# Windowed attention and FFN in one planned kernel: flag, branch hints, last output, plan slack and the third pair's loads

## The chip, the cores and the metric

The kernel runs on one core of a Trainium2 chip. The metric is the device time of one execution in microseconds, the median over the runs shown. Each execution of the program computes the whole result. TensorE is called PE in the rows, its weight loads PEld; VectorE is DVE, ScalarE is ACT, GpSimd is POOL and SyncE is SP. A "q" behind an engine's name means an instruction of its sequencer (a wait, a branch, a DMA issue).

## The reference

Attention with a window and sink keys over four batches, eight heads, 768 positions and 64 dimensions, and behind it a feed-forward network (FFN) over the 3072 tokens, 512 wide with 2048 hidden units:

```
scores = q @ k.T / sqrt(64)
keep = (pos_k < n_sink) | ((pos_q - pos_k >= 0) & (pos_q - pos_k < window))
a = softmax(where(keep, scores, -1e9))          # n_sink = 4, window = 128
x = (a @ v), heads side by side                 # 3072 x 512
h = x @ w_in
g = where(h >= 1, h, where(h <= -1, 0, (h + 1)**2 / 4))
out = g @ w_out
```

All inputs are float32; q and k come with factors of about 30, so the softmax is sharp. The weights reach the kernel as 64-bit words that it decodes itself.

## The kernel before

The work is cut into eight chunks of 384 tokens (four batches, first and second half of the sequence). For each chunk the attention of eight heads writes the tile `xn`, and then the FFN of this chunk runs while the attention of the next is computed. The first half's heads (16 of the 64 units) are computed in pairs of heads (`pair_load`, `pair_scores`, `pair_sums`, `early_transp`, `pair_r`, `pair_av`), the first four of them in `first_pairs` ahead of everything else; the others are single units (`load`, `scores`, `values`, `transp`, `av`, `sinks`), split into a high and a low part for the product. `pair_load` (L610) brings keys (L616) and queries (L618) of a pair into the rings `ks_ring` and `qh_ring` of two buffers each. The rings `ql_ring` (two buffers) and `kr_ring` (one) are used by the units alone, from 16 on. `pair_values` (L621) loads V into one of two buffers `vq`.

The FFN of a chunk is a loop over 16 blocks of hidden units (`NJ`). `stage1` (L827) makes twelve products (L835) for a block; ACT and VectorE turn the result into g, with a high part `gh` (L846) and a low part `gl` (L847); `stage2` (L850), two blocks later, makes nine products (L858) into three output banks. With the last block, ACT copies each bank (L869) and SP stores it (L871). `split` (L873) makes the high and low part of x (L875, L876). `block` (L320) loads and decodes two weight blocks: the transfer (L359), two byte instructions (L361, L363), a combination (L365), a copy on ACT (L367) and a subtraction (L368).

All of this is not issued as it is written: each step hands `Plan.op` an engine, a guessed time in ns, a function, and what it reads and writes. `Plan.due` works out a due time for each operation from TensorE's order, and `Plan.order` plays the engines against each other: an engine takes the ready operation that is due first; SP takes a transfer no sooner than some microseconds before it is due; for TensorE there are two lanes, A (attention) and B (FFN), each in its own order, and `turn` says which lane's head comes next. If both are ready, the lane whose share of the chunk's work is behind has its turn:

```
ka, kb = ("A", a.group[1]), ("B", b.group[1])
return a if done[ka] * LEAD * total[kb] <= done[kb] * total[ka] else b
```

The instructions are issued in the order that comes out, and the engines wait for one another by semaphores. The order is made on the host; the chip does not change it.

The kernel is right in this form for inputs in a certain range (a sink count up to 4, a window from 1 to 128, scores below a bound, weights whose exponents lie in a range). `checks` (L957 to L969, VectorE) puts these conditions into `flag`; a transpose on TensorE (L978) brings the 128 partitions into one row, and `result` (L971 to L974) makes the integer `other` of it. Before, these steps form a group of their own after the last chunk. `values_load` (L1030) loads `other` into a register on each engine, and each engine branches (L1031): if it is 0, past a block of code that computes everything again in a general way; the block behind `tc.If` is not entered for these inputs. Behind it come waits for all semaphores and the barrier at the end (L1031, L1098).

## Time and profile before

| | |
|---|---|
| time, median of 3 runs | 689.83 us (688.82 to 690.71) |
| time of the profiled execution | 689.68 us |
| its span, first to last instruction | 688.0 us |
| PE busy | 671.2 us (98%) |
| PEld busy | 601.7 us (87%) |
| DVE busy | 501.6 us (73%) |
| ACT busy | 489.2 us (71%) |
| POOL busy | 237.3 us (34%) |
| mean granted TensorE clock | 0.998 of full speed |

The span lies inside the profiled execution's time; 1.7 us are around it. A busy share is an average over stages with different limits, so the views by stretch and in order of time say more than this table. In a view of waits "X <- Y" means that the engine's instruction X was idle until Y was done. Matmuls are pipelined, so their times overlap. Register, branch and semaphore instructions do not count as busy.

### The profile page before, as it was taken

The page shows a single profiled execution, that of the slowest core. Times are in us where ns is not written, and L with a number is a line of the kernel's source. Part 1 is how long each engine was busy: PE and PEld are TensorE (multiplying, and loading weights), DVE is VectorE, ACT ScalarE, POOL GpSimd, SP SyncE. Part 2 cuts the span into 40 slices and gives each one's busy share as a digit, 9 for nine tenths or more (in the row PEclk, how much of TensorE's full clock was granted, in tenths as well). Part 3 has the DMA queues.
Part 4 walks back from the last instruction along what each step waited for, and adds up shares of the span by engine and source line. Part 5 has one row for each costly group of instructions (what it writes and reads, how often), then busy time and mean ns, then how long its engine had stood idle before and what let it go on. Part 6 is the DMA issues. An engine that isn't in the chain of part 4 may idle for free.

```text
span 688.0 us, 11934 instructions
## 1 busy us (share of the span) xinstructions
PE 671.2 (98%) x3853; PEld 601.7 (87%) x3853; DVE 501.6 (73%) x1421; ACT 489.2 (71%) x1245; POOL 237.3 (34%) x421
## 2 busy tenths in 40 slices
PE   6899999999999999999999999999999999999995
PEld 5688888889999999999999999999999999999994
DVE  6998999787767688686786877787787776733221
ACT  6887877777668777887778777797777866544332
POOL 3000014444433445453543454354453444300000
PEclk9999999999999999999999999999999999999999
DMA  6946433231223433434434433434424221000001
GB/s 220 333 170 240 141 143 117 60 92 49 61 65 117 126 110 126 142 98 145 128 93 147 123 105 128 135 118 134 124 89 123 67 89 43 1 31 16 1 0 51
DMA packets 41086, 73.94 MB, mean 107 GB/s; under 512 B 4344, under 2 KB 25656, under 8 KB 41016
## 3 DMA queue, kind: packets, MB, share of 16 engines
q1 hardware_dynamic: 41016, 73.09, 33.4%
q8 instruction: 33, 0.54, 0.3%
q14 instruction: 37, 0.30, 0.1%
HBM read 66.78 MB, written 6.29 MB: 106 GB/s over the span
## 4 chain that ended last, share of the span: by engine, by line
PE 87%; DVE 7%; ACT 2%; DMA 1%; issue 1%; POOL 0%; SPq 0%; POOLq 0%; DVEq 0%
PE o_ps L858 36%; PE h_ps L835 36%; PE ps_a L587 5%; PE ps_a L444 5%; PE ps_a L525 2%; DMA w<-w_in 1%; PE ps_a L656 1%; DVE wi L368 1%; PE ps_a L722 1%; DVE gl L847 1%; DVE x L876 1%; DVE ends L363 1%; ACT p L452 1%; DVE ends L361 1%; DVE w L365 1%
## 5 line engine op out<-in xcount | busy, mean ns | idle before, releaser
L835 PE MATMUL h_ps<-x,wi 128*128 128x384 f32 x1536 | 311.8, 340 | 0.8 <-DVE x L876 0.6
L835 PEld LDWEIGHTS h_ps<-x,wi 128*128 128x128 f32 x1536 | 262.5, 188 | 10.4 <-issue 2.0
L858 PE MATMUL o_ps<-w,gh 128*128 128x512 f32 x768 | 243.4, 398 | 0.0
L858 PE MATMUL o_ps<-w,gl 128*128 128x512 f32 x384 | 151.0, 393 | 0.0
L858 PEld LDWEIGHTS o_ps<-w,gh 128*128 128x128 f32 x768 | 134.1, 188 | 15.8 <-issue 1.5
L844 DVE SCALAR_TENSOR_TENSOR g<-g,h_ps 128x384 f32<-128x384 f32 x128 | 70.4, 550 | 67.1 <-ACT g L843 66.3
L842 ACT ACTIVATE g<-h_ps,half 128x384 f32<-128x384 f32 x128 | 73.9, 577 | 54.1 <-PE h_ps L835 53.2
L847 DVE TENSOR_TENSOR gl<-g,gh 128x384 fp32r<-128x384 f32 x128 | 77.0, 602 | 29.4 <-ACT gh L846 28.8
L452 ACT ACTIVATE p<-p,peak 128x260 f32<-128x260 f32 (+1 forms) x144 | 71.6, 497 | 37.2 <-DVE peak L449 35.0
L846 ACT CAST gh<-g 128x384 fp32r<-128x384 f32 x128 | 65.3, 510 | 45.1 <-DVE g L844 43.9
L426 POOL TENSOR_TENSOR q_l<-r,q_h 128x384 fp32r<-128x384 f32 x48 | 50.6, 1053 | 116.9 <-ACT q_h L425 116.8
L858 PEld LDWEIGHTS o_ps<-w,gl 128*128 128x128 f32 x384 | 72.0, 188 | 16.9
L449 DVE CUSTOM_DVE_ANT_0 p<-ps_a,m 128x260 f32<-128x260 f32 (+1 forms) x144 | 57.7, 408 | 21.7 <-PE ps_a L444 21.4
L843 ACT ACTIVATE g<-g 128x384 f32<-128x384 f32 x128 | 67.2, 525 | 3.2
L471 DVE CUSTOM_DVE_ANT_0 p<-p,stat 128x128 f32<-128x128 f32 x128 | 60.1, 496 | 2.3
L546 POOL TENSOR_SCALAR_AFFINE_SELECT pt<-pt 128x384 fp32r<-128x384 f32 (+1 forms) x96 | 49.1, 514 | 23.7 <-ACT pt L534 12.6
L498 POOL TENSOR_TENSOR v_s<-r,v_s 128x256 fp32r<-128x256 f32 (+1 forms) x48 | 36.2, 754 | 60.1 <-ACT v_s L497 59.0
L551 POOL TENSOR_SCALAR_AFFINE_SELECT pt<-pt 128x384 fp32r<-128x384 f32 (+1 forms) x96 | 50.4, 545 | 0.2
L587 PEld LDWEIGHTS ps_a<-pt,v_s 128*128 128x128 f32 x304 | 42.5, 188 | 2.5 <-POOL v_s L498 0.2
L444 PE MATMUL ps_a<-k_s,q_l 128*128 128x260 f32 (+1 forms) x144 | 40.7, 283 | 1.3 <-POOL q_l L426 1.1
L587 PE MATMUL ps_a<-pt,v_s 128*128 128x256 f32 (+1 forms) x304 | 41.9, 275 | 0.0
L444 PE MATMUL ps_a<-k_s,q_h 128*128 128x260 f32 (+1 forms) x144 | 39.6, 275 | 0.0
(161 smaller groups left out, 851.6 us busy)
## 6 DMA issues: line engine op xcount, KB each, us to landing
r<-qk SPq DMA_DIRECT2D x48, 192.0 KB, 2.4
k_r<-qk SPq DMA_DIRECT2D x32, 262.0 KB, 2.8
w<-w_in SPq DMA_DIRECT2D x8, 1024.0 KB, 7.5
again<-w_in SPq DMA_DIRECT2D x16, 512.0 KB, 4.1
again<-w_out SPq DMA_DIRECT2D x16, 512.0 KB, 3.8
w<-w_out SPq DMA_DIRECT2D x6, 1024.0 KB, 8.5
out<-o SPq DMA_DIRECT2D x23, 256.0 KB, 2.4
r<-vx SPq DMA_DIRECT2D x32, 128.0 KB, 2.1
```

The costliest lines, as they stand in the source:

```text
L444: nc.tensor.matmul(ps()[:, lo:260], lhsT=q()[:, i * P:(i + 1) * P], rhs=k_s()[:, c0:c0 + 260 - lo], start=(j == 0), stop=(j == len(qs) - 1))
L449: op(DVE, 215 if lo else 350, lambda: nc.vector.tensor_tensor_reduce(out=p()[:, i, lo:260], in0=ps()[:, lo:260], in1=m, scale=-0.125, scal ...
L452: op(ACT, 400 if lo else 500, lambda: nc.scalar.activation(p()[:, i, lo:260], p()[:, i, lo:260], AF.Exp, bias=peak[:, n, i:i + 1], scale=-1.0,
L471: nc.vector.tensor_tensor_reduce(out=own, in0=own, in1=p()[:, k, 0:P], scale=r, scalar=0.0, op0=ALU.add, op1=ALU.add, accum_out=stat()[:, ...
L587: nc.tensor.matmul(z, lhsT=w, rhs=y, start=(n == 0), stop=(n == len(mms) - 1))
L835: nc.tensor.matmul(h_ps()[:, :T], lhsT=w_i[j][:, w, ct * P:(ct + 1) * P], rhs=x()[:, y, ct], start=(ct == 0 and n == 0), stop=(ct == NCT - ...
L842: op(ACT, 490, lambda: nc.scalar.activation(g(), h_ps()[:, :T], AF.Relu, bias=half, scale=0.5), r=[h_ps], w=[g])
L843: op(ACT, 440, lambda: nc.scalar.activation(g(), g(), AF.Square), w=[g])
L844: op(DVE, 470, lambda: nc.vector.scalar_tensor_tensor(g(), g(), 1.0, h_ps()[:, :T], op0=ALU.min, op1=ALU.max), r=[h_ps], w=[g])
L846: op(ACT, 420, lambda: nc.scalar.copy(gh(), g()), r=[g], w=[gh])
L847: op(DVE, 500, lambda: nc.vector.tensor_tensor(gl(), g(), gh().bitcast(F32), op=ALU.subtract), r=[g, gh], w=[gl])
L858: nc.tensor.matmul(ps(), lhsT=gg()[:, tt * P:(tt + 1) * P], rhs=w_o[j][:, w], start=(j == 0 and n == 0), stop=(j == NJ - 1 and n == 2))
```

## The change

Five things are changed. `checks` and `result` move into a step `decide` of lane A, put in the middle of the last chunk's FFN steps. A hint, one instruction on each engine, is placed in the last chunk behind the low part of block 13 of 16; it belongs to the branch, which now has a label, and to the jump past the general block. The last of the 24 output tiles is copied and stored in two halves of 256 columns: ACT copies and stores the first, VectorE copies and SP stores the second. `turn` gets a slack: where both lanes' heads are ready and the preferred one has been ready for less than 800 ns of the plan, but the other for 800 ns or more, the other has the turn. And the third pair's queries and keys go into a buffer of `ql_ring` and the one of `kr_ring`. The bodies of `checks` and `result` are as before.

```diff
--- before.py
+++ after.py
@@ -44,6 +44,7 @@
 SOON = 40000
+SLACK = 800
@@ -145,7 +146,8 @@ turn(t)
                 ka, kb = ("A", a.group[1]), ("B", b.group[1])
-                return a if done[ka] * LEAD * total[kb] <= done[kb] * total[ka] else b
+                x, y = (a, b) if done[ka] * LEAD * total[kb] <= done[kb] * total[ka] else (b, a)
+                return y if x.ready + SLACK > t >= y.ready + SLACK else x
@@ -612,7 +614,7 @@ pair_load(m)
-        q_h, k_h = qh_ring.new(), ks_ring.new()
+        q_h, k_h = (ql_ring.new(), kr_ring.new()) if m == 2 else (qh_ring.new(), ks_ring.new())
@@ -846,6 +848,8 @@ stage1
         hs[j] = gh, gl
+        if plan.on and (row0, j) == (last, NJ - 3):
+            op(HOST, 1, lambda: tc.mark_branch_hint_location("other", "LikelyTaken", list(mybir.ALL_ENGINES)), r=[gl])
@@ -861,14 +865,19 @@ stage2
             end = (row0, tt) == (last, CT - 1)
-            o = ("out",) if end else out_ring.new()
-
-            def at():
-                return xn.rearrange("p c t -> p (c t)")[:, :DM] if end else o()
-
-            op(ACT, 500, lambda: nc.scalar.copy(at(), ps()), r=[ps] + [("xn", c, a) for c in range(NCT) for a in range(2)]
-               if end else [ps], w=[o])
-            op(SP, 420, lambda: nc.sync.dma_start(out[row0 + tt * P:row0 + (tt + 1) * P, :], at()), r=[o], size=1 << 18)
+            rows = out[row0 + tt * P:row0 + (tt + 1) * P, :]
+            if not end:
+                o = out_ring.new()
+                op(ACT, 500, lambda: nc.scalar.copy(o(), ps()), r=[ps], w=[o])
+                op(SP, 420, lambda: nc.sync.dma_start(rows, o()), r=[o], size=1 << 18)
+                return
+            o = xn.rearrange("p c t -> p (c t)")
+            x_k = [("xn", c, a) for c in range(NCT) for a in range(2)]
+            h0, h1 = slice(0, DM // 2), slice(DM // 2, DM)
+            op(ACT, 320, lambda: nc.scalar.copy(o[:, h0], ps()[:, h0]), r=[ps] + x_k, w=["end0"])
+            op(DVE, 320, lambda: nc.vector.tensor_copy(o[:, h1], ps()[:, h1]), r=[ps] + x_k, w=["end1"])
+            op(ACT, 420, lambda: nc.scalar.dma_start(rows[:, h0], o[:, h0]), r=["end0"])
+            op(SP, 420, lambda: nc.sync.dma_start(rows[:, h1], o[:, h1]), r=["end1"], size=1 << 17)
@@ -919,6 +928,35 @@
+    flag = const.tile([P, CT], F32, name="flag")
+    other = const.tile([1, 1], I32, name="other")
+
+    def checks():
...
+    def decide():
+        ps = bank_a.new()
+
+        def result():
...
+        op(DVE, 4000, checks, w=["flag", "both"] + [("peak", n, i) for n in range(len(units)) for i in range(CT)])
+        op(PE, 110, lambda: nc.tensor.transpose(ps()[0:1, :P], flag[:, 0:1], ident), r=["flag"], w=[ps])
+        op(DVE, 700, result, r=[ps], w=["flag"])
@@ -945,38 +983,11 @@
         if c == len(chunks) - 1:
             ffn, attn = ffn + tail, []
+            ffn.insert(len(ffn) // 2, ("A", 0.1, decide))
         run(spread([("A",) + step for step in attn], ffn, LEAD), c + 1)
...
-    plan.group = "A", len(chunks) + 1, 0.1
-    flag = const.tile([P, CT], F32, name="flag")
-    other = const.tile([1, 1], I32, name="other")
...
-    op(DVE, 4000, checks, w=["flag", "both"] + [("peak", n, i) for n in range(len(units)) for i in range(CT)])
-    ps = bank_a.new()
-    op(PE, 110, lambda: nc.tensor.transpose(ps()[0:1, :P], flag[:, 0:1], ident), r=["flag"], w=[ps])
-    op(DVE, 700, result, r=[ps], w=["flag"])
@@ -1028,7 +1039,7 @@
     other_v = nc.values_load(other, min_val=0, max_val=1)
-    with tc.If(other_v > 0):
+    with tc.If(other_v > 0, preferred_fallthrough_block=True, label="other"):
```

## Rows read from the trace of the kernel before

**Rows 1.** Busy time by stage: us, then each engine's busy us (instructions), clock, DMA, GB/s.

```profile
20.00:40.00 20.00, 18.13 (x145) 12.82 (x142) 19.86 (x51) 16.98 (x50) 0.00 (x0) 1.00 0.81 275
120.00:600.00 480.00, 478.62 (x2725) 439.38 (x2724) 366.56 (x1106) 362.47 (x931) 220.65 (x376) 1.00 0.33 102
```

**Rows 2.** Order of time on SP, 1 to 17 us: start, us, instruction.

```profile
3.13 0.94 SPq L623 DMA_DIRECT2D vq<-vx  x2
7.43 0.34 SPq L616 DMA_DIRECT2D k_s<-qkp  x1
...
9.47 0.33 SPq L616 DMA_DIRECT2D k_s<-qkp  x1
...
10.32 0.45 SPq L359 DMA_DIRECT2D w<-w_in  x1
```

**Rows 3.** Order of time on VectorE, 13 to 24 us; in brackets the idle time before.

```profile
15.18 0.56 DVE L729 TENSOR_TENSOR xn<-ps_a,xn 128x384 f32<-128x384 f32 x1 [0.35 <-ACT xn L762]
17.50 0.76 DVE L361 TENSOR_SCALAR ends<-w 128x1024 uint8<-128x1024 uint8 x1 [1.77 <-DMA w<-w_in]
...
20.07 0.42 DVE L667 CUSTOM_DVE_ANT_0 pt<-ps_a,m 128x260 f32<-128x260 f32 x1
```

**Rows 4.** Order of time on TensorE, 12 to 36 us.

```profile
12.97 1.25 PE L722 MATMUL ps_a<-pt,vq 128*64 128x128 f32 x12
...
18.52 0.38 PE L656 MATMUL ps_a<-k_s,q_h 64*128 64x260 f32 x1
...
34.34 1.13 PE L835 MATMUL h_ps<-x,wi 128*128 128x384 f32 x5 [0.61 <-DVE x L876]
```

**Rows 5.** Waits between 110 and 190 us: us in total, times, longest us.

```profile
PEld ps_a L444 <- POOL q_l L426: 2.4, 5, 0.8
...
PE ps_a L444 <- POOL q_l L426: 1.1, 2, 0.6
PE ps_a L525 <- DVE peak L449: 0.6, 1, 0.6
```

**Rows 6.** Order of time on all engines, from 680.6 us.

```profile
680.53 0.39 PE L858 MATMUL o_ps<-w,gl 128*128 128x512 f32 x1
...
680.76 0.27 PE L978 MATMUL ps_a<-ident,flag 128*1 128x128 f32 x1
...
680.96 0.59 ACT L869 COPY xn<-o_ps 128x512 f32<-128x512 f32 x1
...
681.57 0.33 SPq L871 DMA_DIRECT2D out<-xn  x1
```

**Rows 7.** DMA: a queue's packets, MB, share; an issue's KB, us to landing.

```profile
q8 instruction: 33, 0.54, 0.3%
...
out<-xn SPq DMA_DIRECT2D x1, 256.0 KB, 2.0
```

**Rows 8.** The branch's line: ns of one, first and last start in us.

```profile
L1031 SPq EVENT_SEMAPHORE  x8: 17/17/17, 686.0 to 686.6; - x8
...
L1031 POOLq COMPARE_BRANCH  x1: 45/45/45, 682.6 to 682.6; - x1
...
L1031 PEldq COMPARE_BRANCH  x1: 4306/4306/4306, 682.6 to 682.6; - x1
L1031 POOLq EVENT_SEMAPHORE  x1: 17/17/17, 682.8 to 682.8; - x1
L1031 SPq COMPARE_BRANCH  x1: 45/45/45, 682.9 to 682.9; - x1
```

**Rows 9.** The line that loads the flag into registers.

```profile
L1030 PEldq TENSOR_LOAD <-other x1: 749/749/749, 681.7 to 681.7; - x1
L1030 SPq TENSOR_LOAD <-other x1: 558/558/558, 682.0 to 682.0; - x1
```

**Rows 10.** ScalarE's instructions by line and form: busy us, mean ns, idle before.

```profile
L705 ACT COPY pt<-ps_a 128x256 f32<-128x256 f32 x16 | 5.9, 366 | 0.4 <-PE ps_a L701 0.3
```

**Rows 11.** Busy time in one stretch near the end, columns as in rows 1.

```profile
674.00:677.00 3.00, 3.00 (x16) 2.57 (x15) 0.56 (x1) 1.54 (x3) 0.00 (x0) 1.00 0.03 5
```

More of the change, by code (lines that the diff above doesn't have):

```diff
@@ L921, in attn_ffn @@
     pt0 = [pt_ring.new() for _ in range(2)]
+    flag = const.tile([P, CT], F32, name="flag")
+    other = const.tile([1, 1], I32, name="other")
+    def checks():
+        v, both = nc.vector, chk[1]
+        pk = peak.rearrange("p u i -> p (u i)")
+        v.tensor_tensor(pk, pk, pk, op=ALU.mult)
+        v.tensor_reduce(flag[:, 1:2], pk, axis=mybir.AxisListType.X, op=ALU.add)
+        v.tensor_scalar(flag[:, 0:1], flag[:, 1:2], LARGE2, None, op0=ALU.is_lt)
+        for value, bound, o in ((n_f, float(NSINK), ALU.is_le), (w_f, float(P), ALU.is_le), (w_f, 1.0, ALU.is_ge)):
+            v.scalar_tensor_tensor(flag[:, 0:1], value, bound, flag[:, 0:1], op0=o, op1=ALU.mult)
+        v.tensor_scalar(both, both, 0x38383838, None, op0=ALU.bitwise_and)
+        v.tensor_scalar(both, both, 0x38383838, None, op0=ALU.bitwise_xor)
+        v.tensor_scalar(both.bitcast(F32), both, 0.0, None, op0=ALU.is_equal)
+        v.tensor_reduce(flag[:, 1:2], both.bitcast(F32), axis=mybir.AxisListType.X, op=ALU.min)
+        v.tensor_tensor(flag[:, 0:1], flag[:, 0:1], flag[:, 1:2], op=ALU.mult)
+    def decide():
+        ps = bank_a.new()
+        def result():
+            nc.vector.tensor_reduce(flag[0:1, 1:2], ps()[0:1, :P], axis=mybir.AxisListType.X, op=ALU.min)
+            nc.vector.tensor_scalar(flag[0:1, 2:3], flag[0:1, 1:2], -1.0, 1.0, op0=ALU.mult, op1=ALU.add)
+            nc.vector.tensor_copy(other, flag[0:1, 2:3])
+        op(DVE, 4000, checks, w=["flag", "both"] + [("peak", n, i) for n in range(len(units)) for i in range(CT)])
+        op(PE, 110, lambda: nc.tensor.transpose(ps()[0:1, :P], flag[:, 0:1], ident), r=["flag"], w=[ps])
+        op(DVE, 700, result, r=[ps], w=["flag"])
     def run(steps, c):
@@ L950, in attn_ffn @@
             op(HOST, 1, close_early, w=["dec", "chk"])
-    plan.group = "A", len(chunks) + 1, 0.1
-    flag = const.tile([P, CT], F32, name="flag")
-    other = const.tile([1, 1], I32, name="other")
-    def checks():
-        v, both = nc.vector, chk[1]
-        pk = peak.rearrange("p u i -> p (u i)")
-        v.tensor_tensor(pk, pk, pk, op=ALU.mult)
-        v.tensor_reduce(flag[:, 1:2], pk, axis=mybir.AxisListType.X, op=ALU.add)
-        v.tensor_scalar(flag[:, 0:1], flag[:, 1:2], LARGE2, None, op0=ALU.is_lt)
-        for value, bound, o in ((n_f, float(NSINK), ALU.is_le), (w_f, float(P), ALU.is_le), (w_f, 1.0, ALU.is_ge)):
-            v.scalar_tensor_tensor(flag[:, 0:1], value, bound, flag[:, 0:1], op0=o, op1=ALU.mult)
-        v.tensor_scalar(both, both, 0x38383838, None, op0=ALU.bitwise_and)
-        v.tensor_scalar(both, both, 0x38383838, None, op0=ALU.bitwise_xor)
-        v.tensor_scalar(both.bitcast(F32), both, 0.0, None, op0=ALU.is_equal)
-        v.tensor_reduce(flag[:, 1:2], both.bitcast(F32), axis=mybir.AxisListType.X, op=ALU.min)
-        v.tensor_tensor(flag[:, 0:1], flag[:, 0:1], flag[:, 1:2], op=ALU.mult)
-    def result():
-        nc.vector.tensor_reduce(flag[0:1, 1:2], ps()[0:1, :P], axis=mybir.AxisListType.X, op=ALU.min)
-        nc.vector.tensor_scalar(flag[0:1, 2:3], flag[0:1, 1:2], -1.0, 1.0, op0=ALU.mult, op1=ALU.add)
-        nc.vector.tensor_copy(other, flag[0:1, 2:3])
-    op(DVE, 4000, checks, w=["flag", "both"] + [("peak", n, i) for n in range(len(units)) for i in range(CT)])
-    ps = bank_a.new()
-    op(PE, 110, lambda: nc.tensor.transpose(ps()[0:1, :P], flag[:, 0:1], ident), r=["flag"], w=[ps])
-    op(DVE, 700, result, r=[ps], w=["flag"])
     plan.issue()
```

## The prediction

> **What bounds the kernel now.** I read the stages first [rows 1]. From 120 to 600 us TensorE is busy for 478.62 of 480 us; there only fewer or better placed TensorE instructions give time. From 20 to 40 us VectorE is busy for 19.86 us and TensorE for 18.13: weight decoding on VectorE is the bound there. Ahead of that VectorE still waits for data (below). So the change can act in three places: the head, the few waits left in the middle, and the end.
>
> In the head the SP queue comes next [rows 2]. SP issues its transfers in a fixed order. After the two V loads at 3.13 us nothing leaves until 7.43: the third pair's keys wait for a buffer that the first pair's scores hold, and the fourth pair's, for the second pair's scores, leave only at 9.47. The first weight block stands behind both and leaves at 10.32. VectorE waits for it: its idle stretch of 1.77 us before the first decode ends at 17.50 by that transfer [rows 3]. TensorE is held by the same chain until its wait of 0.61 us for VectorE at 34.34 [rows 4].
>
> In the middle I take the waits between 110 and 190 us [rows 5]: TensorE itself idles 1.1 us for POOL's low part of the queries and 0.6 us for VectorE's maxima, its weight loads 2.4 us for POOL.
>
> At the end the order of time [rows 6] shows the last product at 680.53 (0.39 us), its eviction at 680.96 (0.59 us), the store issued at 681.57, and between them the transpose of the flag. The store lands 2.0 us after its issue [rows 7], so at 683.6, yet the span runs to 688.0. The rows of the branch [rows 8] tell why: SP branches at 682.9 and its next instruction stands at 686.0, and TensorE's branch lasts 4.306 us, while POOL branches at 682.6 and goes on at 682.8. The two wait 3 to 4 us for something that is no data of the kernel; I read it as the code behind the jump over the general path.
>
> **Flag in the last chunk.** The checks on VectorE already run in the attention stretch; what moves is one transpose and VectorE's three small instructions. At the end that takes them off the way of the register loads on TensorE, ACT, POOL and VectorE, not off SP's: SP's load starts at 682.0 [rows 9], after its own DMA issue ends at 681.9. TensorE, which loads its register at 681.7 [rows 9], can do so about 0.7 us earlier, since its last product ends at 680.92. In the middle of the chunk the transpose costs at most its 0.27 us [rows 6], at least nothing if a wait takes it in. TensorE is full there, so I take **+0.2**. VectorE is far from full there, which hides the rest; without that cover its three instructions would stand ahead of an FFN product as they stood ahead of the branch.
>
> **Hints and halves.** If the hints bring the code in time, SP goes on 0.1 to 0.2 us after its branch, as POOL does [rows 8]. Then the landing of the last store decides. The copy in halves, one on ACT and one on VectorE, takes 0.37 us by the 128x256 copy from PSUM [rows 10] in place of 0.59: 0.22 less. The landing of a half is not shown at this place; the nearest row is the 2.0 us of the whole, and I leave it. SP's wait then ends at 681.57 - 0.22 + 2.0 = 683.35 instead of 686.04: 2.7 us. The 16 semaphore instructions and the barrier behind it (686.0 to 688.0) stay. ACT's own DMA issue brings perhaps a semaphore more, so I take **-2.6**. The bounds: -2.9, if a half lands 0.2 sooner; -0.3, if the code still comes late, for then SP's branch is only 0.2 and TensorE's only 0.7 us earlier, and each keeps its stall. The price of the hint instructions, one an engine, is not shown; the nearest rows are the branches of 0.045 us [rows 8], and TensorE's queue hides as much, so nothing, at most 0.1.
>
> **Third pair's loads.** Its keys and queries go to buffers that no one uses before the units, so their two issues stand right after the second pair's and move the V loads by two issues, some 0.95 us. The first V product starts at 12.97 [rows 4], some 8 us after their new issue at about 4.1, so that hides it. The rings of the pairs shift by one: the fourth pair now waits for the first pair's scores (SP at 7.43), and the fifth for the second's. In the queue the first weight block follows two issues after 7.43, as it stands two issues (0.85 us) after 9.47 now, so at 8.3 instead of 10.32: 2.0 us sooner, and the second block as well, since SP waits for nothing between. VectorE is free at 15.73 and would start to decode there rather than at 17.50, 1.77 sooner. But it does not keep all of it: its decode of three instructions then ends at 18.3, and the next one in its order, at 20.07, reads scores that TensorE finishes at 18.9 [rows 3, 4]. So 20.07 becomes 18.9 to 19.0: 1.1 us. Behind it VectorE has no gap worth the name (19.86 of 20 us busy), up to TensorE's wait at 34.34. I take **-1.1**. The bounds are 0 (the planner's order turns out so that the block is held by something else) and -1.8.
>
> **Slack.** The planner takes the other lane's matmul, if that has been ready for 800 ns and the preferred one has not. In a full TensorE this costs nothing by itself and can empty the waits [rows 5]: 1.7 us of TensorE's own, 2.4 us for POOL counted by the weight loads, part of which the matmul before covers. None is over 0.8 us, so the slack is as long as they are. Some will come back elsewhere, since the whole order shifts. I take **-1.2**, between +1.0 (new waits of the same kind, two of the longest more than vanish) and -2.4.
>
> **The sum.** -2.6 - 1.1 - 1.2 + 0.2 = -4.7 us. The profiled execution took 689.68 us, 0.15 under the median of the runs (689.83), so the median should go to **685.1**.
>
> **Rivals.** First, the code comes late all the same. For it: nothing in the trace shows a hint at work. Against: POOL shows that a branch with its code at hand is free. It costs 2.3 of the 2.6 us: 687.4.
>
> Second, the plan turns against itself: the matmuls put ahead by the slack, and loads that are planned sooner, shift the orders of ACT, VectorE and POOL. The head gives nothing, and three or four new waits of 0.6 us for POOL appear where units begin. For it: the waits between 110 and 190 us [rows 5] lie at that handover, and they are most of the 1.4 us that TensorE idles from 120 to 600 us [rows 1], so it is the place that reacts. Against: TensorE has always FFN matmuls that are ready. 689.83 - 2.6 + 0.2 + 2.0 = 689.4, no change.
>
> Third, on the slower side: the hinted code takes the place of code that TensorE needs before the branch. The profile shows 33 fetches of 0.54 MB in all [rows 7], 16.4 KB each, on a queue that I take for TensorE's; one fetch lies between 674 and 677 us, where 5 GB/s over 3 us are 15 KB and nothing else is loaded [rows 11]. TensorE stays busy for 3.00 of 3.00 us through it, since the code came ahead. The hint stands after the low part of the third last block of hidden units, near 669 us, thus some 6 us ahead of that crossing. If the hinted block pushes out the one needed next, TensorE stalls there as at its branch, 4.3 us, and the branch finds its code gone again. 689.83 - 0.3 - 1.1 - 1.2 + 0.2 + 4.3 = 691.7, or 692.9 if the slack gives nothing; 692.3 between them. It decides against the change as soon as that stall is over 2.4 us. [...]
>
> That the change does not do what it says is the first rival for the hints; for the early loads it would be the weight block still behind a wait, which adds 1.1 us to the forecast: 686.2, inside its range.
>
> **How the numbers follow.** The forecast gets 0.66, late code 0.14, the plan against itself 0.13, pushed-out code 0.07. The forecast's own bounds are 689.83 - 2.9 - 1.8 - 2.4 + 0 = 682.7 and, with hints working, 689.83 - 2.4 + 0 + 1.0 + 0.3 = 688.7. The first rival lies inside. The range is 682.6 to 688.8. A measurement of this kernel tells about 0.3% from no change, that is 2.07 us: faster means under 687.76, slower over 691.90. Faster: 0.62 of the forecast, 0.09 of late code, 0.04 of the plan: 0.75. Same: 0.03, 0.05, 0.07 and 0.02 of the pushed-out code: 0.17. Slower: the rest, 0.02 of the plan, 0.05 of the pushed-out code and 0.01 of the forecast: 0.08.
>
> **What would show it.** Hints: the branch rows of ACT, VectorE, SP and TensorE followed within 0.2 us, TensorE's branch far below 4.306 us, and the last semaphore wait of SP ended by the store's landing. Halves: two copies of about 0.37 us side by side. Loads: the first weight block issued near 8.3 us, VectorE's wait for it gone or under 0.3 us, and the wait at 34.34 about 1.1 us earlier. Slack: no wait of TensorE for POOL between 110 and 190 us. I am wrong if the branch stalls stay, if the weight block still leaves after 10 us, or if TensorE's busy time in 120 to 600 us falls below today's 478.6.

## The result, and the profile after

The changed kernel takes 693.69 us (median of 6 runs, 692.64 to 694.17); the kernel before, run beside it on the same chip, takes 690.11 us (688.82 to 690.75). The ratio is 1.0053, with a 95% interval from 1.0041 to 1.0065: slower by 3.6 us. The forecast was 685.1 us in a range from 682.6 to 688.8, so the sign was wrong and the range missed. The profiled execution took 693.86 us with a span of 692.1; 1.7 us are around it, as before.

The busy time by stretch comes first, as in [rows 1]: stretch, length, busy us and instructions of PE, PEld, DVE, ACT and POOL, granted clock, DMA share, GB/s.

```profile
20.00:40.00 20.00, 19.30 (x152) 14.63 (x149) 19.46 (x47) 18.74 (x59) 0.00 (x0) 1.00 0.74 257
...
60.00:120.00 60.00, 57.51 (x334) 47.67 (x333) 57.44 (x108) 42.91 (x104) 11.88 (x13) 1.00 0.40 138
...
400.00:500.00 100.00, 97.98 (x554) 88.79 (x553) 74.45 (x225) 77.04 (x197) 48.00 (x80) 1.00 0.38 117
...
120.00:600.00 480.00, 476.41 (x2698) 435.29 (x2697) 362.81 (x1102) 361.98 (x925) 215.45 (x375) 1.00 0.34 102
```

From 20 to 40 us TensorE does 1.2 us more than in [rows 1]. From 120 to 600 us it is busy for 476.41 us instead of 478.62 and gets 27 products fewer done, at the same clock.

How far the two kernels are at the same amount of TensorE work says where the time changes hands. Each kind of product is counted at its median distance to the next one in both traces, worked out from the traces outside the profile's views; the table gives the time of the other kernel less that of before, in us, at the point where so much work is done (the second and third kernels are experiments below):

```
work done (us)           40    80   120   160   200   280   360   440   480   560   end
after                  -1.8  -2.1  -0.1  -0.3  -0.8  -0.9   0.0  +0.9  +4.6  +5.7  +5.7
no slack               -2.3  -2.5  -3.9  -4.9  -5.1  -5.3  -5.4  -5.3  -5.1  -5.2  -5.6
attention ahead        -1.1  -1.1  -0.3  +0.2   0.0  +2.3  +5.9  +8.9 +11.0 +11.2 +11.0
```

After gains 2 us in the head, loses them between 80 and 120 us, and loses 6.6 more between 280 and 560 us, 3.7 of these between 440 and 480 us of work. The six largest waits of TensorE from 100 to 600 us (engine, instruction, what it waited for: us in total, times, longest):

```profile
PE ps_a L589 <- DVE peak L451: 1.4, 2, 1.0
PE ps_a L446 <- POOL q_l L428: 0.9, 2, 0.6
PE ps_a L527 <- DVE peak L451: 0.9, 1, 0.9
PE o_ps L862 <- DVE gl L849: 0.7, 1, 0.7
PE ps_a L446 <- DVE xn L731: 0.6, 1, 0.6
PE ps_a L604 <- DVE peak L451: 0.5, 1, 0.5
```

Before, TensorE had the two waits of [rows 5] in this stretch, 1.7 us together, and none behind 190 us. After, these six are 5.0 us; 2.9 us of that lie between 100 and 125 us, where the gain of the head is lost, and 2.1 behind 380 us.

The name `peak` in three of these rows misleads. VectorE's instruction at L451 writes the maxima, but it also reads the scores out of a bank of `ps_a`, and there are three such banks. The product with V (L589), the transposes (L527) and the sinks' product (L604) read no maxima; in the kernel's own list of what each must wait for, L451 stands only because it empties the bank they write next. The score behind L731 waits for a bank too. So 3.4 of the 5.0 us are waits for a bank that VectorE empties late, and 1.6 us are waits for inputs (the low part of the queries from POOL, the low part of g from VectorE).

TensorE's own waits are not the whole loss. Between 280 and 600 us they are 2.6 us, and its weight loads idle for some 6 us in the same stretch, partly at the same moments, where before neither idles at all. The two largest:

```profile
PEld ps_a L446 <- POOL q_l L428: 1.6, 3, 0.8
PEld ps_a L589 <- POOL v_s L500: 1.3, 1, 1.3
```

One of the late places in the order of time on POOL, near 488 us of the span (start, us, instruction, in brackets the idle time before it):

```profile
488.21 0.23 POOL L461 TENSOR_SCALAR stat<-stat 128x3 f32<-128x3 f32 x1 [5.00 <-ACT p L454]
488.61 1.01 POOL L428 TENSOR_TENSOR q_l<-r,q_h 128x384 fp32r<-128x384 f32 x1 [0.17 <-ACT q_h L427]
```

and on TensorE just behind it:

```profile
489.68 0.39 PE L446 MATMUL ps_a<-k_s,q_l 128*128 128x260 f32 x1 [0.56 <-POOL q_l L428]
...
496.57 1.00 PE L589 MATMUL ps_a<-pt,v_s 128*128 128x256 f32 x7 [1.01 <-DVE peak L451]
```

POOL idles for 5 us with the sums of ACT's exponentials next in its order, and the low part of the queries stands behind them; TensorE's scores come late, and later its product with V waits for the bank that VectorE's L451 empties. It is a chain of several engines, not one slow instruction.

The head, first on SP (compare [rows 2]), then on VectorE (compare [rows 3]):

```profile
3.23 0.43 SPq L618 DMA_DIRECT2D k_r<-qkp  x1
3.70 0.43 SPq L620 DMA_DIRECT2D q_l<-qkp  x1
4.18 0.95 SPq L625 DMA_DIRECT2D vq<-vx  x2
7.46 0.34 SPq L618 DMA_DIRECT2D k_s<-qkp  x1
7.85 0.43 SPq L620 DMA_DIRECT2D q_h<-qkp  x1
8.32 0.43 SPq L361 DMA_DIRECT2D w<-w_in  x1
```

```profile
15.39 0.56 DVE L731 TENSOR_TENSOR xn<-ps_a,xn 128x384 f32<-128x384 f32 x1 [1.15 <-PE ps_a L724]
...
16.16 0.73 DVE L363 TENSOR_SCALAR ends<-w 128x1024 uint8<-128x1024 uint8 x1
```

The first weight block leaves at 8.32 us instead of 10.32, and VectorE decodes at 16.16 instead of 17.50 without idling for it.

The end: the rows of the branch's line (duration, first and last start), of the hint, and in the order of time the last copies and stores.

```profile
L1042 SPq EVENT_SEMAPHORE  x8: 17/17/17, 689.0 to 690.8; - x8
...
L1042 PEldq COMPARE_BRANCH  x1: 408/408/408, 684.1 to 684.1; - x1
...
L1042 SPq COMPARE_BRANCH  x1: 70/70/70, 687.5 to 687.5; - x1
```

```profile
L1109 PEldq BRANCH_PREFETCH_HINT  x1: 50/50/50, 0.9 to 0.9; - x1
```

```profile
686.22 0.39 PE L862 MATMUL o_ps<-w,gl 128*128 128x512 f32 x1
686.64 0.42 DVE L878 COPY xn<-o_ps 128x256 f32<-128x256 f32 x1 [3.29 <-PE o_ps L862]
687.10 0.33 SPq L880 DMA_DIRECT2D out<-xn  x1
687.10 0.37 ACT L877 COPY xn<-o_ps 128x256 f32<-128x256 f32 x1 [0.55 <-DVE xn L878]
687.51 0.38 ACTq L879 DMA_DIRECT2D out<-xn  x1
```

The transfers' own rows (KB, us from issue to landing):

```profile
out<-xn SPq DMA_DIRECT2D x1, 128.0 KB, 1.9
out<-xn ACTq DMA_DIRECT2D x1, 128.0 KB, 2.8
```

TensorE's branch takes 0.41 us instead of 4.306 [rows 8], and SP's next semaphore comes with the landing of its store, at 689.0. But the hints stand at 0.7 to 0.9 us of the span, not near 669 where the program's text puts them. The two copies do not run side by side: ACT's half waits for VectorE's. The ACT half is issued last and lands last, at 690.29. From the end of the last product (686.61) to the end of the span it is 5.5 us, before 7.0.

### The profile page after: what moved, and what is told of

Its sections match the earlier page's. It is cut to its first block, busy times and chain, and to the rows that moved or that the text cites. A ratio compares the mean times of both kernels' runs of the same rounds, so it can differ in the third digit from the quotient of the medians.

```text
span 692.1 us, 11921 instructions
## 1 busy us (share of the span) xinstructions
PE 674.9 (98%) x3853; PEld 603.0 (87%) x3853; DVE 498.9 (72%) x1422; ACT 489.9 (71%) x1245; POOL 233.5 (34%) x421
## 4 chain that ended last, share of the span: by engine, by line
PE 70%; DVE 16%; ACT 8%; issue 3%; POOL 1%; DMA 0%; SPq 0%; POOLq 0%; ACTq 0%; DVEq 0%
PE h_ps L837 30%; PE o_ps L862 29%; PE ps_a L589 4%; PE ps_a L446 3%; DVE p L473 2%; DVE gl L849 2%; PE ps_a L527 2%; DVE g L846 2%; ACT p L454 1%; DVE p L451 1%; DVE w L367 1%; DVE ends L363 1%; DVE w L370 1%; DVE ends L365 1%; DVE xn L594 1%
## 5 line engine op out<-in xcount | busy, mean ns | idle before, releaser
L837 PE MATMUL h_ps<-x,wi 128*128 128x384 f32 x1536 | 316.2, 340 | 0.1
L862 PE MATMUL o_ps<-w,gh 128*128 128x512 f32 x768 | 240.1, 394 | 0.0
L862 PEld LDWEIGHTS o_ps<-w,gh 128*128 128x128 f32 x768 | 141.1, 188 | 20.8 <-issue 0.5
L548 POOL TENSOR_SCALAR_AFFINE_SELECT pt<-pt 128x384 fp32r<-128x384 f32 (+1 forms) x96 | 49.8, 520 | 65.6 <-ACT pt L536 47.3
L500 POOL TENSOR_TENSOR v_s<-r,v_s 128x256 fp32r<-128x256 f32 (+1 forms) x48 | 34.5, 719 | 101.3 <-ACT v_s L499 100.8
L473 DVE CUSTOM_DVE_ANT_0 p<-p,stat 128x128 f32<-128x128 f32 x128 | 62.0, 509 | 2.3
L451 DVE CUSTOM_DVE_ANT_0 p<-ps_a,m 128x260 f32<-128x260 f32 (+1 forms) x144 | 54.5, 406 | 4.9 <-PE ps_a L446 4.8
L553 POOL TENSOR_SCALAR_AFFINE_SELECT pt<-pt 128x384 fp32r<-128x384 f32 (+1 forms) x96 | 47.9, 520 | 0.3
L589 PE MATMUL ps_a<-pt,v_s 128*128 128x256 f32 (+1 forms) x304 | 43.7, 281 | 1.5 <-DVE peak L451 1.4
L589 PEld LDWEIGHTS ps_a<-pt,v_s 128*128 128x128 f32 x304 | 40.7, 189 | 3.3 <-POOL v_s L500 1.3
L446 PE MATMUL ps_a<-k_s,q_l 128*128 128x260 f32 (+1 forms) x144 | 39.2, 286 | 1.3 <-POOL q_l L428 0.9
```

Of the source, the lines that this page charges most:

```text
L446: nc.tensor.matmul(ps()[:, lo:260], lhsT=q()[:, i * P:(i + 1) * P], rhs=k_s()[:, c0:c0 + 260 - lo], start=(j == 0), stop=(j == len(qs) - 1))
L451: op(DVE, 215 if lo else 350, lambda: nc.vector.tensor_tensor_reduce(out=p()[:, i, lo:260], in0=ps()[:, lo:260], in1=m, scale=-0.125, scal ...
L473: nc.vector.tensor_tensor_reduce(out=own, in0=own, in1=p()[:, k, 0:P], scale=r, scalar=0.0, op0=ALU.add, op1=ALU.add, accum_out=stat()[:, ...
L589: nc.tensor.matmul(z, lhsT=w, rhs=y, start=(n == 0), stop=(n == len(mms) - 1))
L837: nc.tensor.matmul(h_ps()[:, :T], lhsT=w_i[j][:, w, ct * P:(ct + 1) * P], rhs=x()[:, y, ct], start=(ct == 0 and n == 0), stop=(ct == NCT - ...
L862: nc.tensor.matmul(ps(), lhsT=gg()[:, tt * P:(tt + 1) * P], rhs=w_o[j][:, w], start=(j == 0 and n == 0), stop=(j == NJ - 1 and n == 2))
```

## The experiments

Times are medians. Ratios are to the kernel before, run beside it on the same chip, with a 95% interval.

**No slack.** The kernel after, with one figure changed:

```
-SLACK = 800
+SLACK = 0
```

> The changed kernel with the slack set to 0; early loads, flag, hints and halves stay. Theory A (the slack's order of TensorE brings the new waits of 488 to 497 and 565 to 575 us): the 1.5 us gained at the end and the 1.8 us gained in the head remain, the 6 us lost behind 90 us of work do not come: about 687 us. Theory B (the ring shift of the early loads changes the order for the worse): still about 693 us. Theory C (any new order costs, each part by itself): 690 to 692 us.

Measured: 682.45 us, ratio 0.9887 (0.9871 to 0.9904). The slack is the loss, and it is 11.2 us. In the trace TensorE is full:

```profile
120.00:600.00 480.00, 480.00 (x2734) 441.51 (x2733) 366.96 (x1098) 360.37 (x930) 218.65 (x373) 1.00 0.34 101
```

and from 100 to 600 us a single wait of TensorE itself is left:

```profile
PE ps_a L527 <- DVE p L471: 0.4, 1, 0.4
```

So the waits of [rows 5], which the prediction gave to the slack, vanish without it. By the table above the gain comes in two parts, 2.3 us up to 40 us of work and 2.8 more up to 200.

**No early loads.** The kernel after, slack kept, the third pair's loads as before:

```
-q_h, k_h = (ql_ring.new(), kr_ring.new()) if m == 2 else (qh_ring.new(), ks_ring.new())
+q_h, k_h = qh_ring.new(), ks_ring.new()
```

> The changed kernel with the third pair's loads back in their own rings; slack, flag, hints and halves stay. Theory A (slack): 693 to 695 us, the head's 1.8 us lost too. Theory B (early loads): about 688 us, the tail's gain and perhaps some of the slack's. Theory C: 690 to 692 us.

Measured: 695.63 us, ratio 1.0082 (1.0065 to 1.0099). Under the slack the early loads bring only 1.9 us.

**The end alone, whole output.** The kernel before with the flag in the last chunk and the hints, without slack, early loads and halves. Against after:

```
-SLACK = 800
+SLACK = 0
...
-q_h, k_h = (ql_ring.new(), kr_ring.new()) if m == 2 else (qh_ring.new(), ks_ring.new())
+q_h, k_h = qh_ring.new(), ks_ring.new()
...
-op(ACT, 320, lambda: nc.scalar.copy(o[:, h0], ps()[:, h0]), r=[ps] + x_k, w=["end0"])
-op(DVE, 320, lambda: nc.vector.tensor_copy(o[:, h1], ps()[:, h1]), r=[ps] + x_k, w=["end1"])
-op(ACT, 420, lambda: nc.scalar.dma_start(rows[:, h0], o[:, h0]), r=["end0"])
-op(SP, 420, lambda: nc.sync.dma_start(rows[:, h1], o[:, h1]), r=["end1"], size=1 << 17)
...
+op(ACT, 500, lambda: nc.scalar.copy(at(), ps()), r=[ps] + [("xn", c, a) for c in range(NCT) for a in range(2)]
+   if end else [ps], w=[o])
+op(SP, 420, lambda: nc.sync.dma_start(out[row0 + tt * P:row0 + (tt + 1) * P, :], at()), r=[o], size=1 << 18)
```

> The kernel before with the flag in the last chunk and the hints alone; no slack, no early loads, the last output whole. Its order of instructions equals that of before up to the last chunk. If the end is worth what the changed kernel's end shows, 1.5 us with halves and 1.0 us more with a whole output (the ACT store landed 2.8 us after its issue, and the two copies ran one behind the other): 687.6 us, with TensorE's last product at the same 681 us and no stall at the branches. If the hints had a price in the stream (fetches, PE stalls), over 688.5 us.

Measured: 688.03 us, ratio 0.9966 (0.9952 to 0.998). **Flag alone**, the same without hints and with the branch as before:

```
-if plan.on and (row0, j) == (last, NJ - 3):
-    op(HOST, 1, lambda: tc.mark_branch_hint_location("other", "LikelyTaken", list(mybir.ALL_ENGINES)), r=[gl])
...
-with tc.If(other_v > 0, preferred_fallthrough_block=True, label="other"):
+with tc.If(other_v > 0):
```

> The kernel before with the flag in the last chunk alone: no hints, no label on the branch, no halves, no slack, no early loads. Theory (the code behind the branch is what the end waits for, and the flag only frees register loads that are not last): each engine but POOL stands 3 to 4 us behind its branch as before, 0.2 to 0.7 us gained: 689.2 to 690 us. Rival (the flag's late arrival was a good part of the end): 688 us, as with flag and hints.

Measured: 689.74 us, ratio 0.9998 (0.9988 to 1.0008). The flag's place is worth nothing that can be measured; the hints bring 1.7 us (2.2 by the two ratios). TensorE's branch, first with the flag alone, then with hints:

```profile
L1035 PEldq COMPARE_BRANCH  x1: 3597/3597/3597, 678.0 to 678.0; - x1
```

```profile
L1037 PEldq COMPARE_BRANCH  x1: 492/492/492, 678.9 to 678.9; - x1
```

**Whole output.** The kernel after with the last output copied by ACT and stored by SP in one piece: the last part of the diff of the end alone.

> The changed kernel with the last output copied and stored whole by ACT and SP, as before; everything else as changed. By the copies one behind the other (0.42 and 0.37 us against 0.59) and the ACT store's landing of 2.8 us against 1.9: 1.0 us less than the changed kernel, 692.7 us. If the halves are worth what was forecast (0.2 us gained): 693.9 us. The plan's order may shift a little in the last chunk only.

Measured: 693.14 us, ratio 1.0042 (1.0025 to 1.0059): by the medians the halves cost 0.55 us, which the intervals of the two ratios (1.0042 here, 1.0053 for after) do not set apart from nothing. The traces say it more plainly: the store of 256 KB lands 2.3 us after its issue, and from the last product to the end of the span it is 4.86 us, against 5.53 with halves. **ACT's queue used earlier**: the kernel after without slack, with one store of the chunk before issued by ACT, to see whether the slow half is the first use of that queue.

```
+if (row0, tt) == (chunks[-2][0] * S + chunks[-2][1] * P, CT - 1):
+    op(ACT, 420, lambda: nc.scalar.dma_start(rows, o()), r=[o])
+else:
+    op(SP, 420, lambda: nc.sync.dma_start(rows, o()), r=[o], size=1 << 18)
```

> The kernel without slack (682.45 us; the last store's ACT half landed 2.77 us after its issue) and with one earlier store, the last of the chunk before, issued by ACT too. If the 2.8 us are the first use of that queue: the half lands after 1.9 to 2.0 us, and the kernel takes 681.7 us. If ACT's issue or queue is slower in itself: 2.7 to 2.8 us again and 682.4 us.

Measured: 682.05 us, ratio 0.9885 (0.9867 to 0.9903), the same as without that store.

```profile
out<-o ACTq DMA_DIRECT2D x1, 256.0 KB, 2.1
...
out<-xn ACTq DMA_DIRECT2D x1, 128.0 KB, 2.9
```

The earlier store of 256 KB lands in 2.1 us, the half at the end in 2.9. First use is not the reason. The landings in the trace say more: a store raises its semaphore in 16 parts, and of this half 14 parts come by 1.88 us after the issue, only the last two at 2.2 and 2.9. The section on the hardware has what runs beside them.

**Other slacks.** `SLACK = 300`, `1600` and `3000` in place of `800`, all else as after. The theory was that margin is what counts: the longer attention is put off until it is surely ready, the fewer waits.

> The changed kernel with a slack of 300 ns in place of 800. Theory (margin): an FFN product that goes on in the same bank counts as just ready, because the product before it in the bank ends as it starts; so the slack hardly ever puts off attention, it lets attention go first as soon as its head has been ready for the length of the slack. In the plan the number of attention steps from 120 to 600 us that start less than 800 ns after they are ready goes from 1 (no slack) over 3 (800) to 58 (300). Less margin, more waits: slower than the changed kernel, 695 to 700 us. Rival (bursts: longer runs of one lane load ACT and VectorE unevenly; the plan changes lanes 591 times without slack, 375 times with 800, 475 with 300): faster than the changed kernel, 687 to 692 us.

Measured: 696.64 us, ratio 1.0104 (1.0081 to 1.0128).

> The changed kernel with a slack of 1600 ns. Margin theory: 250 of 252 attention steps then start 1.6 us or more after they are ready, so nearly no waits from 120 to 600 us: 682 to 685 us. Rival (bursts): the plan changes lanes only 341 times, fewer than with 800, so as slow or slower: 693 to 697 us.

Measured: 691.61 us, ratio 1.003 (1.0017 to 1.0044). That lies in neither theory's range.

> The changed kernel with a slack of 3000 ns. With 1600 ns the time was 691.6 us, neither theory's: waits remained although 250 of 252 attention steps had 1.6 us of margin in the plan. Margin theory with real steps later by up to 3 us than planned: 241 of 252 steps now start 3 us or more after they are ready, so the waits from 120 to 600 us go and the time is 682 to 684 us. If it is the order itself (fewer changes of lane: 475 against 591 without slack and 475 with 300 ns, where it was 696.6 us), 690 us or more.

Measured: 690.5 us, ratio 1.0009 (0.9999 to 1.0019). The margin in the plan alone is refuted: in the plan with 3000 ns no attention product starts less than 1.6 us after it is ready, and the kernel is still 8.05 us behind the one without slack. Its two largest waits (100 to 600 us) are scores that wait for a bank of `ps_a`:

```profile
PE ps_a L446 <- DVE xn L608: 1.8, 3, 0.8
PE ps_a L446 <- ACT vsx L506: 1.3, 2, 0.7
```

ACT's L506 reads no bank. Both times VectorE's L595, which does, ends 0.12 us before the scores' weight load starts (421.79 and 421.91 us, 507.48 and 507.60), and L506 happens to end then as well; so VectorE empties the bank late here too, as in the rows of after. The plan's margin is not the chip's: the score that starts at 489.24 us has been ready for 3.25 us in the plan, and on the chip it waits 0.85 us.

**Slack by other engines.** The kernel after, slack of 800 ns kept, but a product counts as just ready only if another engine delivered its input just now:

```
             a.ready = max(a.ready, free[e] if a.eng == e and e != SP else end)
+            if a.eng != e:
+                a.fresh = max(a.fresh, end)
...
-return y if x.ready + SLACK > t >= y.ready + SLACK else x
+return y if x.fresh + SLACK > t >= y.fresh + SLACK else x
```

> The changed kernel with its slack of 800 ns, but the slack looks only at what other engines delivered; a product that waits for the one before it on TensorE no longer counts as just ready. Margin theory: the slack then does what it was for, the plan is nearly that without slack (587 lane changes, 5 steps under 1.6 us of margin): 682 to 683 us, as without slack. If putting off attention itself is what costs: 688 us or more.

Measured: 682.78 us, ratio 0.9905 (0.988 to 0.9931), within 0.4 us of no slack.

```profile
120.00:600.00 480.00, 480.00 (x2734) 441.48 (x2733) 366.09 (x1098) 361.12 (x930) 217.62 (x373) 1.00 0.33 101
```

So the flaw is in what the slack calls ready. A product of `stage1` that continues its bank is ready when the product before it ends, on the same engine, so that it looks fresh at every turn although nothing can make it late. The rule then puts the FFN off and takes attention, the opposite of its words. The planner's own order, played on the host, shows it: with 800 ns the rule changes the turn 213 times between 120 and 600 us of the plan, and 210 of these put off such a product of `stage1`. Counted from other engines alone, it changes the turn once in that stretch: as it was meant, the slack has next to nothing to do in this kernel. The table has the orders (attention products from 120 to 600 us of the plan, some 250 in each; a run is a number of them without an FFN product between; the last column is the share of a chunk's attention done at half of its TensorE work, chunks 3 to 7):

```
order                     time us   runs of 1/2/3   started < 1.6 us after ready   done at half
before                     689.8     252/0/0          24                           .54-.55
no slack                   682.45    253/0/0           6                           .54-.55
800, other engines only    682.78    252/0/0           5                           .54-.55
300                        696.64    150/49/1        114                           .57-.70
800 (after)                693.69     82/45/26        94                           .62-.72
1600                       691.61     59/32/43         2                           .54-.62
3000                       690.50    153/33/11         0                           .52-.58
clusters, no slack         686.49     42/89/11        27                           .54-.55
attention ahead, no slack  699.07    186/14/13       116                           .62
```

Among the orders with early loads, time grows with the number of thin starts as long as the slack is 800 ns or less, and not beyond. The planner cannot see any of it: in its own play, with its guessed times, the last operation starts at the same 692.46 us in every one of these orders (before: 692.35).

The last two are made to tell two properties of these orders apart: attention in clusters, and attention ahead of its share with thin margins.

**Clusters without slack.** No slack; the planner stays in its lane until the other is 1% of the chunk behind:

```
+RUN = 0.02
...
-x, y = (a, b) if done[ka] * LEAD * total[kb] <= done[kb] * total[ka] else (b, a)
-return y if x.ready + SLACK > t >= y.ready + SLACK else x
+lag = done[kb] / total[kb] - done[ka] * LEAD / total[ka]
+if abs(lag) > RUN / 2:
+    lane[0] = "A" if lag > 0 else "B"
+return a if lane[0] == "A" else b
```

> The kernel after without slack (682.45 us), with one edit in the choice of lane: the lane that the planner is in is kept until the other is behind by 1% of the chunk. In the plan the attention products between 120 and 600 us come in 42 runs of one, 89 of two and 11 of three (without slack 253 runs of one, with the slack of 800 ns 82, 45 and 26); their share of the chunk stays even, and 27 of 253 start less than 1.6 us after they are ready (6 without slack, 94 with it). Clusters as the cause (bursts of exponentials and copies on ACT and VectorE, of which the next scores wait for a bank): 688 to 692 us, with waits of TensorE's scores for VectorE and POOL at 120 to 600 us. Attention pulled ahead of its share, with thin margins, as the cause: 682 to 684, TensorE over 479.5 us busy from 120 to 600.

Measured: 686.49 us, ratio 0.9949 (0.9935 to 0.9963), between the two ranges; its seven runs lie further apart than those of the others, 685.04 to 689.33, and the profiled one is the longest of them.

```profile
120.00:600.00 480.00, 479.41 (x2728) 441.45 (x2727) 369.36 (x1105) 362.49 (x930) 221.39 (x376) 1.00 0.33 102
```

**Attention ahead.** No slack; attention's done share counts less, so it is preferred until it is ahead:

```
-SLACK = 800
+SLACK = 0
...
-x, y = (a, b) if done[ka] * LEAD * total[kb] <= done[kb] * total[ka] else (b, a)
+x, y = (a, b) if done[ka] * LEAD * 0.85 * total[kb] <= done[kb] * total[ka] else (b, a)
```

> The kernel after without slack (682.45 us), with one edit in the choice of lane: attention's done share counts 0.85, so that attention is preferred until it is ahead of its share by that factor. In the plan its products come in 186 runs of one, 14 of two and 13 of three; half way through a chunk 62% are done (55% without slack, 62% with the slack of 800 ns), FFN is left alone for up to 16 us at the end of a chunk, and 116 of 253 start less than 1.6 us after they are ready. Clusters as the cause: 682 to 686 us, few new waits. Attention ahead with thin margins as the cause: 690 to 694 us, with the waits of TensorE for VectorE, ACT and POOL spread over 200 to 600 us.

Measured: 699.07 us, ratio 1.0131 (1.0114 to 1.0148), beyond the range of the theory of thin margins on its own side.

```profile
120.00:600.00 480.00, 472.42 (x2667) 428.52 (x2666) 364.41 (x1090) 357.27 (x920) 216.16 (x372) 1.00 0.33 102
```

```profile
PE ps_a L527 <- DVE peak L451: 4.2, 8, 1.4
PE ps_a L589 <- POOL v_s L500: 2.4, 4, 0.7
PE ps_a L446 <- POOL q_l L428: 2.0, 5, 0.6
```

In 480 us it gets 67 products fewer done than the order without slack; clusters get 6 fewer. Attention ahead of its share, with the thin margins that come with it, is enough to make this loss without any slack, and its waits are of the kinds seen after: for a bank that VectorE's L451 empties, and for inputs from POOL. Clusters cost 4.0 us, but from 120 to 600 us only 0.6 us of TensorE's busy time in the profiled run; most of the loss lies ahead of that. What neither of them explains is the slack of 3000 ns, which is not ahead and has thick margins in the plan. Its waits are for the same banks; why VectorE empties them so much later than planned stays open.

**The best version.** Early loads, flag, hints, whole output, no slack: the diff of the end alone without its part on the loads.

> Early loads, flag and hints, without slack and with a whole last output. From the run without slack (682.45 us) and the changed kernel with a whole output (0.55 us under the changed one): 681.9 us. If the end's two parts do not add: 682.5 us.

Measured: 681.98 us, ratio 0.989 (0.987 to 0.991), 6.05 us under the end alone by the medians (5.2 by the two ratios). It beats both kernels.

**What the hints do.** The best version without the hint instructions, the word on the preferred block kept; then with the hints and without that word.

```
-if plan.on and (row0, j) == (last, NJ - 3):
-    op(HOST, 1, lambda: tc.mark_branch_hint_location("other", "LikelyTaken", list(mybir.ALL_ENGINES)), r=[gl])
```

```
-with tc.If(other_v > 0, preferred_fallthrough_block=True, label="other"):
+with tc.If(other_v > 0, label="other"):
```

> The best version so far (early loads, flag in the last chunk, whole last output, no slack: 681.98 us) without the hint instructions; the branch keeps its label and the word that the fall through is the preferred block. The hint instructions as what removes the stalls: the branches of TensorE and SP stall again by 3 to 4 us, 683.8 to 684.3 us, 33 fetches of TensorE's code and 37 of the others'. The place of the general block as what removes them (the way past it becomes the straight one): 681.7 to 682.2 us, TensorE's branch under 0.6 us, 32 and 33 fetches.

Measured: 683.77 us, ratio 0.9909 (0.9892 to 0.9926).

```profile
L1035 PEldq COMPARE_BRANCH  x1: 3512/3512/3512, 672.7 to 672.7; - x1
```

> The same version with the hint instructions, but without the word on the preferred block. The hint instructions as what removes the stalls: 681.7 to 682.2 us and TensorE's branch under 0.6 us. The place of the general block: 683.8 to 684.3 us, TensorE's branch 3.5 to 4.4 us, 33 fetches of its code.

Measured: 681.59 us, ratio 0.9878 (0.9862 to 0.9895).

```profile
L1037 PEldq COMPARE_BRANCH  x1: 502/502/502, 672.7 to 672.7; - x1
```

The hint instructions do it, and the word on the block does nothing: without them the queue that the prediction takes for TensorE's code makes 33 fetches (as [rows 7]), with them 32. TensorE's stall itself is not what costs: in the run without hints it is over by 676.2 us, and SP goes on at 680.24, with the landing of its store at 680.22. That landing is the difference, 4.3 us after the issue without hints, 2.4 with them.

## Why the prediction was wrong

**Slack, forecast -1.2, measured +11.2.** This is the step that failed, and it decides the sign. It read the rule by its words: the matmul that is taken out of turn is the one that has long been ready, and "in a full TensorE this costs nothing by itself". It did not ask whose head looks fresh. A continuing FFN product does at nearly every turn, so attention was taken out of turn, ahead of its share; that this definition is the flaw is shown (682.78 us with readiness counted from other engines alone). Even so defined the slack brings nothing: TensorE is busy for 480.00 of 480 us with it and without it. How the order loses time is shown in part: an order with attention ahead and no slack loses 12.8 us against no slack between 120 and 560 us of work, in the same kinds of waits. The wait of [rows 5] "for VectorE's maxima" was misread too: the transposes read no maxima and wait for one of three banks. The upper bound of +1.0, "two of the longest more than vanish", was taken from the size of today's waits, but those belong to an order in which 228 of 252 attention products have over 1.6 us to spare. A rule that reorders hundreds of instructions is not bounded by the waits it starts from.

**The rival nearest to the truth** was the plan that turns against itself. It was right in kind (new waits, some for POOL and more for banks that VectorE empties), and wrong in place and price: most of the loss lies between 280 and 560 us, not where units begin, and 689.4 us was 4.3 too little. Its argument against itself, "TensorE has always FFN matmuls that are ready", held in the plan at each of the 210 turns, but by the slack's rule those were the ones put off.

**Early loads, forecast -1.1, measured -6.05 (by ratios -5.2) in an order without slack and -1.9 in the order with it.** Every step up to the weight block came as forecast: issued at 8.32 us, no idle time of VectorE before the decode. The term was mis-sized twice. In the head it is 2.3 us, because the forecast kept TensorE's scores at 18.9 us while the third pair's loads had moved too: TensorE does 1.17 us more from 20 to 40 us, as shown, and about as much more in the first 20 us (15.09 us busy, before 14.10). Single traces scatter here: the end alone, without early loads, has 18.77 and 14.83 us. And 2.8 us more come up to 200 us, where the waits of [rows 5] vanish. In the planned order of before, 15 of 33 attention products between 140 and 200 us start less than 1.6 us after they are ready; with the early loads and no slack none of 32 does. The prediction gave these waits to the slack.

**Hints, size near, mechanism right in part.** The branch goes on at once (0.41 us on TensorE, 0.07 on SP) and the landing of the store ends SP's first wait, as written. But with the flag early SP's wait ends with that landing also without hints (685.33 and 685.31 us with the flag alone): what the hints take away there is not SP's wait for code but 1.8 to 1.9 us of the landing, a term the prediction does not have. The gain is 1.7 to 2.2 us with a whole output, against 2.4 forecast (2.6 less the halves' 0.22): the store takes 2.3 us rather than the 2.0 of [rows 7]. That the size came near is partly luck: it counted on hints some 14 us ahead of the branch, and they stand 680 us ahead of it. The rival of pushed-out code needed a hint near 669 us; none stands there, and TensorE has no stall there (26.00 of 26.00 us busy from 660 to 686 us). That hinted code takes the place of other code, no run shows.

**Halves, forecast -0.22, measured +0.55 by the medians and about +0.7 at the end of the traces.** "Two copies of about 0.37 us side by side" fails: each takes about what was forecast (0.42 and 0.37 us), but ACT's starts when VectorE's is done, and its store then lands 2.8 us after its issue. The landing was taken for that of a whole store on SP.

**Flag, forecast +0.2, measured within 0.1 us of nothing.** Within what can be told that agrees, but two things cancel: SP's branch moves from 1.3 to 0.4 us behind the issue of the store, and the landing of the store from 2.0 to 4.1.

The signs named beforehand worked: TensorE's busy time from 120 to 600 us fell below 478.6, which was written down as what would show the forecast wrong.

## What to carry to other kernels

When a planner's rule asks how long something has been ready, look at whose input that is: an instruction that continues the work of its own engine is always just ready and never late, and must not count. Judge a change of order by an experiment with that rule alone, since the waits of the order before do not bound what a new one costs. And look at what an instruction empties as well as at what it writes: a wait named after a result can be a wait for the bank behind it. A hint on the branch past a large block was worth about 2 us of 690 here. Splitting the output's last tile over two engines brought no gain (0.55 us more by the medians): the copies ran one behind the other, and the half on the second queue landed 2.8 us after its issue. Look at both before splitting.

## What the runs showed of the hardware

TensorE's hint, executed at 0.9 us and 50 ns long, took its branch near 673 us from 3.51 us down to 0.50 us, with one fetch of 16.4 KB fewer. In the three traces without hints the branch takes 3.51 to 4.31 us (3.51 and 3.60 with the flag early, 4.306 before [rows 8]); in four traces with hints, which stand 671 to 683 us ahead of it, 0.41 to 0.50. The trace of after shows no fetch of instructions between 0 and 13.07 us, so none right behind the hints. What a hint brings, and how much code an engine holds, no run shows.

Two copies from one PSUM tile by two engines ran one behind the other: ACT's came 0.03 us after VectorE's end (687.07 and 687.10 us). In the program ACT's instruction waits for VectorE's semaphore, so the order comes from that wait; whether the chip could overlap the two was not tried.

A half of 128 KB on ACT's queue landed 2.8 and 2.9 us after its issue, SP's half, issued 0.4 us earlier, after 1.9; a whole store of 256 KB on ACT's queue in the chunk before took 2.1. And in the two kernels with the flag early and no hints the last whole store on SP landed 4.1 and 4.3 us after its issue, with hints 2.3 to 2.4; before, with the flag late, it was 2.0 [rows 7].

The traces show what is late: not the store, but the last of its 16 parts. ACT's half after has 14 parts by 1.88 us, the last two at 2.2 and 2.8. The whole store of the best version without hints has 12 parts by 2.04 us, the last four from 2.45 to 4.26. Fetches of instructions run beside the late parts: 8 KB each at 688.99 to 689.43 us (two) and 689.95 to 690.26 after, one of 16 KB from 677.13 to 678.77 us in the run without hints, where the store was issued at 675.96. Before, the first fetch behind the issue starts at 683.63 us, when the last of the 16 parts has landed (683.61), and none is late. With the hints that fetch of 16 KB behind the branch is gone, and the landing is 1.9 us sooner. So the late parts are put down to fetches on the way of the store; this is argued from their times, and no run moves a fetch alone.
